# Attention of a fused attention and expert kernel: unsplit 4-byte products on halves of the array

## The chip, the cores and the metric

The kernel runs on one core of a Trainium2 chip. The metric is the device time of one execution in microseconds. A core has TensorE (PE; its weight loads are listed as PEld), VectorE (DVE), ScalarE (ACT), GpSimd (POOL) and SyncE (SP, which issues the DMAs), each with its own instruction queue.

## What is computed

```python
# q, k, v: (B=2, H=8, S=576, D=64), float32
scores = matmul(q, k.T) / sqrt(D) + bias[h]      # bias: a small network of |i - j| and i, the same for both batches
attn   = exp(scores - max);  attn /= attn.sum(-1) + 1e-9
x      = matmul(attn, v)                         # put together to (B*S=1152, H*D=512)
x = max(x @ w1, x @ w2, x @ w3) @ w_out          # first dense layers, 768 wide
P = softmax-like gate of x (8 Sinkhorn rounds over 1152 tokens and 8 experts)
out = sum_e P[:, e] * (relu(x @ w1_e) @ w2_e)    # 8 experts, 1024 wide
```

All of it is held to nearly float32 precision. The kernel gets there by splitting operands: hi is the operand rounded to float32r, lo is the rest, and a product is the sum of two or three products of such halves.

## The kernel before

Stages follow one another: the bias table (loop over 36 groups of 16 rows, written to DRAM as `bias_f`), attention, the first dense layers (`m1_mm`, L661), their output product (L1037), the gate (L1082 is its product) and the experts (L1186, L1276), which fill the time from some 380 us on. Every engine runs its instructions in the order in which the program gives them (`manual_schedule`); the loops below therefore fix the order of each queue.

Attention goes through 72 units, 9 per head: unit k < 8 is query block k // 2 (128 rows) of batch k % 2, unit 8 is the last 64 rows of both batches. In step s of the loop (L691) these follow: `u_qk(s)` (L463): scores of unit s into a tile `sc`, two halves of 288 keys. The stationary operand `qs` holds q hi on rows 0 to 63 of the array and q lo on rows 64 to 127, so that one matmul with `kh` and one with `kl` per key half do the whole product. `u_tr(s - 3)` (L557) transposes four key blocks of 128 of the exponentials through TensorE into `pt`, `u_trl` (L565) the last 64 keys, the key tail, into `pl`. `u_max(s - 1)` (L485, VectorE) adds the bias and takes the row maximum, `u_exp(s - 2)` (L499, ACT) the exponential and its row sum. `u_ev(s - 4)` (L578) takes `pt` apart into hi `pth` (ACT copy, L575) and lo `ptl` (VectorE subtraction, L576). `pv_mm` (L604) multiplies with `vs`, which holds v hi on 64 columns and v lo on the other 64, in 9 matmuls per batch and query half of 256 or 320 rows; `pv_ev` (L617) adds the two column halves, partly by way of a DMA and GpSimd. `prep_head` (L178, GpSimd) splits q, k and v of the next head. The row sums' inverses go through a transpose (L521) and DRAM and come back as factors for `x_out` (L644); for the last head `r_mm` (L546) spreads them over the array. `m1_first` (L668) places 36 matmuls of the dense layers into the drain of the attention loop, and `w_step` (L135) prepares their weights. For head 0, GpSimd does the splits in five pieces inside the bias loop (L430, one of them on ACT).

Tiles in flight: `sc` 2 buffers of two banks each, `pt` 2, `pl` 1, `pv` 1, `bias` 4.

Of the kernel before, what the change touches and what calls it, by code (L numbers as in the profile page):

```python
# [37 lines left out]
W_AT = (0, 3, 6)  # L38
NEARLY = (3, 3, 0, 0, 3, 0, 3)
LASTV = 2  # L40
NW2 = 0
# [14 lines left out]
def make_body(stop=None):  # L56
    def body(tc, a):
# [21 lines left out]
        with ctx, tc.manual_schedule():  # L79
# [77 lines left out]
            qs = [hp_.tile([128, B, 640], F32R, name=f"qs{p}", bufs=1) for p in range(2)]  # L157
            kt = [[hp_.tile([128, B, S], F32R, name=f"k{x}{p}", bufs=1) for x in "hl"] for p in range(2)]
            vs = [hp_.tile([128, B, 5, 128], F32R, name=f"vs{p}", bufs=1) for p in range(2)]
            for p in range(2):  # L160
                G.memset(raw(qs[p][:, 0, 576:640]), 0.0)
            raw_t = {}
            bias_t = {}

            def load_head(h, part=None):
                if h < H:
                    if not part:
                        raw_t[h] = (hp_.tile([128, 2, B, S], F32, tag="qk", name="qk"),
                                    hp_.tile([128, B, 5, D], F32, tag="vr", name="vr"))
                    qk, vr = raw_t[h]  # L170
                    if part is None:
                        dma(qk, a["qk"][h])
                    elif part < 2:
                        dma(qk[:, part], a["qk"][h][:, part])
                    if part in (None, 2):
                        dma(vr, a["v"][h])

            def prep_head(h, step, b=None, on_act=False):  # L178

                p = h % 2  # L180
                qk, vr = raw_t[h]
                bs = slice(0, B) if b is None else slice(b, b + 1)
                if step[0] == "q":
                    rows = slice(0, 128) if step[1] == "h" else slice(64, 128)
                    out = hi = qs[p][rows, bs, 0:S]
                    src = qk[rows, 0, bs]
                elif step[0] == "k":
                    out, hi = kt[p]["hl".index(step[1])][:, bs], kt[p][0][:, bs]
                    src = qk[:, 1, bs]
                else:  # L190
                    m = lambda x: x.rearrange("p b j d -> p (b j) d")
                    oh = 64 * (h % 2)
                    ol = 64 - oh
                    v = m(vs[p][:, bs])
                    hi = v[:, :, oh:oh + D]
                    out = hi if step[1] == "h" else v[:, :, ol:ol + D]
                    src = m(vr[:, bs])
                if step[1] == "l":
                    G.tensor_tensor(out=out, in0=src, in1=raw(hi), op=ALU.subtract)
                elif on_act:  # L200
                    A.activation(out=out, in_=src, func=AF.Copy)
                else:
                    pool_copy(out, src)

            def load_bias(m):
                h, it = divmod(m, 5)
# [9 lines left out]
            with ExitStack() as bctx:  # L216
# [10 lines left out]
                load_head(0)  # L227
# [185 lines left out]
                for g16 in range(NG16):  # L413
# [13 lines left out]
                    if g16 in (3, 5, 7):  # L427
                        load_head(1, (3, 5, 7).index(g16))
                    if g16 % 4 == 3 and 7 < g16 < 28:
                        prep_head(0, *pieces.pop(0))  # L430
# [18 lines left out]
            with ExitStack() as actx:  # L449
# [74 lines left out]
                def r_out(h):  # L524

                    A.activation(out=rt[0][0:9], in_=st_t.pop(h)[0:9, 256:384], func=AF.Copy)
                    if h == H - 1:
                        r_last.append(rt[0])
                        return
# [839 lines left out]
```

## Time and profile before

| | us |
|---|---|
| median of 3 runs (1098.21 to 1100.75) | 1099.62 |
| profiled execution, its own time | 1099.56 |
| span of the profiled execution, first to last instruction | 1097.8 |
| bias stage, to the first score | 69.0 |
| attention loop, first score to the end of the last | 125.4 |
| drain of attention, to the first dense matmul that isn't moved ahead | 16.55 |
| TensorE busy, of the span | 1049.3 |

How to read the rows: a row of the timeline has start, duration, engine, line, operation, out<-in, the size of the stationary operand, the shape of the moving one and a count of records. Matmuls overlap in the pipeline, so their durations say less than the distance from one start to the next; a row of x4 lasts from the first start to the last end. A row of the windows has the stretch, its length, and for PE, PEld, DVE, ACT and POOL the busy time and the number of records, then the granted TensorE clock (1.00 is 2.4 GHz), the share of DMA time and GB/s. A row of the groups has, behind the count, the busy time in us and the mean ns of one, then the idle time ahead of them and what ended it.

### The profile page before, as it was taken

The page shows a single profiled execution, that of the slowest core. Times are in us where ns is not written, and L with a number is a line of the kernel's source. Part 1 is how long each engine was busy: PE and PEld are TensorE (multiplying, and loading weights), DVE is VectorE, ACT ScalarE, POOL GpSimd, SP SyncE. Part 2 cuts the span into 40 slices and gives each one's busy share as a digit, 9 for nine tenths or more (in the row PEclk, how much of TensorE's full clock was granted, in tenths as well). Part 3 has the DMA queues.
Part 4 walks back from the last instruction along what each step waited for, and adds up shares of the span by engine and source line. Part 5 has one row for each costly group of instructions (what it writes and reads, how often), then busy time and mean ns, then how long its engine had stood idle before and what let it go on. Part 6 is the DMA issues. An engine that isn't in the chain of part 4 may idle for free.

```text
span 1097.8 us, 18483 instructions
## 1 busy us (share of the span) xinstructions
PE 1049.3 (96%) x7160; PEld 737.1 (67%) x7160; DVE 799.5 (73%) x1559; ACT 587.4 (54%) x999; POOL 407.9 (37%) x286
## 2 busy tenths in 40 slices
PE   6779999999999888999999999999999999999998
PEld 3269898999989663656657557566575575665753
DVE  8999999689776678677576676675766766757633
ACT  7989889533333664544535435445454354454530
POOL 6996997122212432252313312313223124132220
PEclk8999999999999899999999999999999999999999
DMA  5888664234413121121212212212112112110002
GB/s 184 275 243 267 218 194 118 67 109 115 85 52 136 25 61 42 41 64 39 63 40 63 63 24 59 67 35 63 45 56 64 24 59 72 30 44 7 1 1 87
DMA packets 41045, 90.61 MB, mean 83 GB/s; under 512 B 8255, under 2 KB 11390, under 8 KB 40062
## 3 DMA queue, kind: packets, MB, share of 16 engines
q1 hardware_dynamic: 40814, 89.14, 28.1%
q8 instruction: 56, 0.92, 0.4%
q10 hardware_dynamic: 144, 0.29, 0.1%
q14 instruction: 31, 0.25, 0.1%
HBM read 75.33 MB, written 13.30 MB: 81 GB/s over the span
## 4 chain that ended last, share of the span: by engine, by line
PE 72%; DVE 17%; ACT 4%; issue 3%; POOL 2%; DMA 1%; DVEq 0%; ACTq 0%; SPq 0%; POOLq 0%
PE d L1276 32%; PE x L1186 12%; PE y L1186 8%; PE z L1186 8%; PE sc L476 3%; PE pv L614 2%; PE pt L562 2%; PE m L665 2%; PE o L1037 2%; POOL s L350 1%; DVE ww L117 1%; DVE ww L112 1%; DVE ww L115 1%; DVE ng L493 1%; DVE ptl L576 1%
## 5 line engine op out<-in xcount | busy, mean ns | idle before, releaser
L1276 PE MATMUL d<-w2h,hl 128*128 128x512 f16 x576 | 218.3, 379 | 0.2 <-DVE hl L1207 0.2
L1276 PE MATMUL d<-w2h,hh 128*128 128x512 f16 x576 | 218.3, 379 | 0.0
L1276 PE MATMUL d<-w2l,hh 128*128 128x512 f16 x576 | 218.3, 379 | 0.0
L1186 PEld LDWEIGHTS <-w1h 128*128 128x128 f16 x1792 | 175.9, 98 | 53.1 <-issue 5.2
L1276 PEld LDWEIGHTS <-hh 128*128 128x128 f16 x1152 | 112.8, 98 | 131.5 <-issue 0.4
L1202 ACT ACTIVATE hh<-s 128x576 f16<-128x576 f32 x128 | 87.4, 683 | 127.1 <-DVE s L1198 101.6
L945 POOL TENSOR_TENSOR w1l<-wf,w1h 128x768 f16<-128x768 f32 x32 | 55.2, 1724 | 257.0 <-ACT w1h L944 239.2
L1207 DVE SCALAR_TENSOR_TENSOR hl<-s,hh 128x576 f16<-128x576 f32 x128 | 109.5, 857 | 49.1 <-ACT hh L1202 46.4
L1291 DVE SCALAR_TENSOR_TENSOR acc<-d,kh,acc 128x512 f32<-128x512 f32 x126 | 94.0, 746 | 67.3 <-PE d L1276 66.8
L1254 POOL TENSOR_TENSOR w2l<-w2r,w2h 128x512 f16<-128x512 f32 x64 | 77.1, 1214 | 117.3 <-ACT w2h L1253 117.3
L1186 PEld LDWEIGHTS <-w1l 128*128 128x128 f16 x896 | 88.3, 99 | 22.9
L1276 PEld LDWEIGHTS <-hl 128*128 128x128 f16 x576 | 56.4, 98 | 68.5 <-DVE hl L1207 0.7
L951 POOL TENSOR_TENSOR w1l<-wf,w1h 128x1024 f16<-128x1024 f32 x32 | 69.7, 2179 | 71.7 <-ACT w1h L948 71.7
L932 ACT ACTIVATE wf<-wr,pw 128x1024 f32<-128x1024 f32 x32 | 36.5, 1141 | 95.0 <-DVE pm L780 95.0
L1198 DVE SCALAR_TENSOR_TENSOR s<-z,cx,s 128x576 f32<-128x576 f32 x64 | 52.3, 817 | 44.4 <-ACT s L1194 28.3
L1194 ACT ACTIVATE s<-x,cx 128x576 f32<-128x576 f32 x96 | 70.2, 731 | 25.8 <-PE x L1186 25.7
L1186 PE MATMUL x<-xth,w1h 128*128 128x288 f16 x384 | 78.5, 286 | 1.2 <-ACT s L1194 1.2
L948 ACT ACTIVATE w1h<-wf 128x1024 f16<-128x1024 f32 x32 | 33.6, 1050 | 84.5 <-DVE wf L941 84.5
L1186 PE MATMUL x<-xth,w1l 128*128 128x288 f16 x384 | 78.7, 287 | 0.0
L1186 PE MATMUL x<-xtl,w1h 128*128 128x288 f16 x384 | 78.7, 287 | 0.0
L665 PE MATMUL m<-xh,wl 128*128 128x384 f32 x216 | 73.9, 342 | 2.5 <-POOL wl L120 2.5
L665 PE MATMUL m<-xh,wh 128*128 128x384 f32 x216 | 74.0, 343 | 1.6 <-ACT wh L119 0.8
(220 smaller groups left out, 2368.4 us busy)
## 6 DMA issues: line engine op xcount, KB each, us to landing
wr<-in_moe_w SPq DMA_DIRECT2D x50, 512.0 KB, 4.4
w2r<-in_moe_w SPq DMA_DIRECT2D x64, 256.0 KB, 2.7
bias_f<-bo SPq DMA_DIRECT2D x36, 295.5 KB, 3.6
bias<-bias_f SPq DMA_DIRECT2D x32, 288.0 KB, 3.0
qk<-in_qk SPq DMA_DIRECT2D x7, 1152.0 KB, 6.3
wr<-in_moe_w_out SPq DMA_DIRECT2D x6, 512.0 KB, 3.6
vr<-in_v SPq DMA_DIRECT2D x8, 320.0 KB, 5.8
bias<-bias_f SPq DMA_DIRECT2D x16, 144.0 KB, 5.1
```

What stands on the lines that cost most here:

```text
L665: T.matmul(out=p[:, :TG], lhsT=ws[:, 128 * c:128 * c + 128], rhs=xs[:, c, TG * g:TG * g + TG], start=(c == 0 and n == 0), stop=(c == 3 and ...
L932: A.activation(out=t[:, 0:4], in_=w1r.pop(n), func=AF.Identity, scale=w_pow[n // 2, 1][:, 2:3])
L945: G.tensor_tensor(out=lo[:, 0:3], in0=t[:, 1:4], in1=hi[:, 0:3], op=ALU.subtract)
L951: G.tensor_tensor(out=lo[:, 3:7], in0=t[:, 4:8], in1=hi[:, 3:7], op=ALU.subtract)
L1186: T.matmul(out=ps[bank][:, s, :SH], lhsT=ws[:, i, c, :], rhs=xs[:, j, c, s * SH:s * SH + SH], start=(start and k == 0), stop=(k == 5), **kw)
L1194: A.activation(out=t, in_=src, func=AF.Identity, scale=c)
L1198: V.scalar_tensor_tensor(out=out, in0=z, scalar=scale, in1=out, op0=ALU.mult, op1=ALU.add)
L1202: A.activation(out=o, in_=src, func=AF.Relu)
L1207: V.scalar_tensor_tensor(out=l, in0=src, scalar=0.0, in1=o, op0=ALU.max, op1=ALU.subtract)
L1254: G.tensor_tensor(out=lo, in0=r, in1=hi, op=ALU.subtract)
L1276: T.matmul(out=pd, lhsT=hs[:, fh, 128 * t:128 * t + 128], rhs=ws, start=(k == 0), stop=(k == 11))
L1291: V.scalar_tensor_tensor(out=acc[:, t, :], in0=pd, scalar=kh[:, 1 + t:2 + t], in1=acc[:, t, :], op0=ALU.mult, op1=ALU.add)
```

## The change

q and k of a head are loaded once per head as one tile, batch 0 on partitions 0 to 63 and batch 1 on 64 to 127, and are used unsplit; so are v and the exponentials. The loop has 36 iterations, 9 per pair of heads, and an iteration n holds two units e: for i = n % 9 < 8 the two batches of query block i // 2 of head 2p + i % 2, for i = 8 the two heads, with the last 64 rows of both batches. Scores of the two batches stand on the two row halves of the array; outputs of the two heads on its two column halves; the key tail of v, exponentials and i = 8's scores on its quarters. Key tails are turned by a plain matmul with the identity, because their result belongs on a column half. ACT and VectorE copy the transposed exponentials in turn; nothing is split. `prep_head`, the pieces in the bias stage, the second sum of outputs and its DMAs are gone.

The diff, cut to its core:

```diff
-NEARLY = (3, 3, 0, 0, 3, 0, 3)
+NEARLY = {36: 3, 38: 3, 39: 3, 40: 3}
...
             def load_head(h, part=None):
                 if h < H:
...
+                    if part in (None, 0):
+                        qk_t[h] = hp_.tile([128, 2, S], F32, tag="qk", name="qk", bufs=4)
+                        dma(qk_t[h], a["qk"][h])
+                    if part in (None, 1):
+                        v_t[h] = hp_.tile([128, B, 5, D], F32, tag="v", name="v", bufs=4)
+                        dma(v_t[h], a["v"][h])
-            def prep_head(h, step, b=None, on_act=False):
...
-                for step in ("qh", "kh"):
-                    prep_head(0, step, on_act=True)
-                pieces = [("ql", 0), ("ql", 1), ("kl", 0), ("kl", 1), ("vh", None, True)]
...
-                    if g16 % 4 == 3 and 7 < g16 < 28:
-                        prep_head(0, *pieces.pop(0))
+                    if g16 in (3, 5, 7, 9):
+                        load_head((g16 - 3) // 2 % 2, (g16 - 3) // 4)
...
+                GW = (512, 512, 128)
+                pts = [[pt_p.tile([128, 4, w], F32, name=f"pt{g}{e}") for e in range(2)] for g, w in enumerate(GW)]
+                ptt = [pt_p.tile([128, w], F32, name=f"ptt{g}") for g, w in enumerate(GW)]
+                NP = 9 * (H // 2)
...
+                def u_qk(n):
+                    p, i = divmod(n, 9)
+                    sc = [ps_s.tile([128, 2, 512], F32, tag="sc", name="sc") for _ in range(2)]
                     for hf in range(2):
+                        ks = slice(hf * SH, hf * SH + SH)
+                        for e in range(2):
+                            if i < 8:
+                                it, r = i // 2, slice(64 * e, 64 * e + 64)
+                                qk = qk_t[2 * p + i % 2]
+                                T.matmul(out=sc[e][:, hf, :SH], lhsT=qk[r, 0, 128 * it:128 * it + 128],
+                                         rhs=qk[r, 1, ks], start=True, stop=True)
+                            else:
+                                qk = qk_t[2 * p + e]
+                                for b in range(B):
+                                    r = slice(64 * b, 64 * b + 64)
+                                    T.matmul(out=sc[e][r, hf, :SH], lhsT=qk[r, 0, 512:576], rhs=qk[r, 1, ks],
+                                             start=True, stop=True)
...
+                            out = r_last[u // 4][o, 128 * (u % 4):128 * (u % 4) + 128] if u < 8 else pl_t[0][o, 128:256]
+                            T.matmul(out=out, lhsT=ident[0:18, 9 * e + u:9 * e + u + 1].to_broadcast([18, 64]),
+                                     rhs=rt[H // 2 - 1][0:18], start=True, stop=True)
...
-                    T.transpose(pl_t[0][0:64, q:q + 128], un[u]["pe"][:, 512:576], ident)
+                    T.matmul(out=pl_t[0][64 * hh:64 * hh + 64, q:q + 128], lhsT=un[u]["pe"][:, 512:576], rhs=ident,
+                             start=True, stop=True)
...
+                def ev(eng, out, in_):
+                    if eng is A:
+                        A.activation(out=out, in_=in_, func=AF.Copy)
+                    else:
+                        V.tensor_copy(out=out, in_=in_)
...
+                def pv_mm(p, g, i0, i1):
...
+                    w = GW[g] // 2
                     for i in range(i0, i1):
+                        b, j = divmod(i, 5)
+                        for e in range(2):
+                            o = slice(64 * e, 64 * e + 64)
+                            c = slice(b * w, b * w + w)
+                            v = v_t[2 * p + e]
+                            if j < 4:
+                                T.matmul(out=ps[o, c], lhsT=v[:, b, j, :], rhs=pts[g][e][:, j, c], start=(j == 0), stop=False)
+                            else:
+                                T.matmul(out=ps[o, c], lhsT=v[o, b, 4, :], rhs=ptt[g][o, c], start=False, stop=True)
...
+                PV = {6: (0, 0, 4), 7: (0, 4, 8), 8: (0, 8, 10), 10: (1, 0, 5), 11: (1, 5, 10), 12: (2, 0, 10)}
+                PV_EV = {8: (0, A), 11: (1, V), 12: (2, A)}
+                L_EV = {5: (0, V), 9: (1, A), 10: (2, V)}
+                TAILS = {1: (), 2: (), 3: (0, 1), 4: (2,), 5: (3,), 6: (), 7: (4, 5), 8: (6,), 9: (7,), 10: (8,), 11: ()}
+                X_OUT = {16: 0, 18: 1}
...
+                for n in range(NP + 6):
+                    if n < NP:
+                        u_qk(n)
+                    if 0 <= n - 2 < NP:
+                        for e in range(2):
+                            u_tr((n - 2, e))
+                    for p, (g, i0, i1) in of(PV, n):
+                        pv_mm(p, g, i0, i1)
+                    for p, tails in of(TAILS, n):
+                        for i in tails:
+                            for e in range(2):
+                                u_trl((9 * p + i, e))
+                    for p, _ in of({11: 0}, n):
+                        r_tr(p)
+                    if 0 <= n - 2 < NP:
+                        u_ev((n - 2, 0), A)
+                    if n < NP:
+                        for e in range(2):
+                            u_max((n, e))
+                            u_exp((n, e))
+                    if 0 <= n - 2 < NP:
+                        u_ev((n - 2, 1), V)
...
+                    m1_first(NEARLY.get(n, 0))
+                    if n == NP + 2:
                         r_mm()
+                for b in range(B):
+                    x_last(b)
```

In the tables the key counts from the pair's first iteration, 9p: `PV` gives group (0 and 1: 256 query rows of each batch, 2: the last 64) and the part of its 10 products. `of` yields the pairs for which a key falls on n.

## Rows read from the trace of the kernel before

**Rows 1.** The page: span, and TensorE's busy time, share and instructions.

```profile
span 1097.8 us, 18483 instructions
...
PE 1049.3 (96%) x7160; PEld 737.1 (67%) x7160; DVE 799.5 (73%) x1559; ACT 587.4 (54%) x999; POOL 407.9 (37%) x286
```

**Rows 2.** One tile's instructions, `sc`: ns min/median/max, first and last start in us.

```profile
L476 PE MATMUL sc<-kh,qs x160: 288/297/607, 69.0 to 194.1; 128*128 128x288 f32 x160
```

**Rows 3.** Windows: heads 0, 1 and 4 of attention, and the gating product.

```profile
68.99:80.82 11.83, 11.35 (x70) 10.02 (x71) 9.95 (x23) 9.17 (x23) 9.98 (x7) 0.86 0.92 278
80.82:96.07 15.25, 15.25 (x123) 15.06 (x123) 14.63 (x34) 13.88 (x34) 9.12 (x6) 1.00 0.90 299
...
127.20:144.50 17.30, 16.04 (x123) 15.02 (x123) 16.94 (x37) 14.84 (x35) 15.35 (x11) 1.00 0.72 213
...
378.38:380.44 2.06, 2.06 (x34) 0.78 (x33) 0.76 (x1) 1.83 (x3) 0.16 (x1) 1.00 0.00 0
```

**Rows 4.** Timeline of TensorE in the attention loop, around 130 and 193 us.

```profile
129.62 0.60 PE L562 MATMUL pt<-ident,pe 128*128 128x128 f32 x4
130.05 0.27 PE L571 MATMUL pl<-ident,pe 128*64 128x128 f32 x1
...
130.63 0.28 PE L614 MATMUL pv<-ptl,vs 128*128 128x256 f32 x1
130.75 0.28 PE L614 MATMUL pv<-pth,vs 128*128 128x256 f32 x1
130.88 0.29 PE L476 MATMUL sc<-kh,qs 128*128 128x288 f32 x1
131.01 0.29 PE L476 MATMUL sc<-kl,qs 128*128 128x288 f32 x1
...
192.88 0.31 PE L614 MATMUL pv<-pth,vs 128*128 128x320 f32 x1
193.02 0.31 PE L614 MATMUL pv<-ptl,vs 128*128 128x320 f32 x1
```

**Rows 5.** Timeline of TensorE around the gating product.

```profile
378.04 0.41 PE L1186 MATMUL x<-xth,w1l 128*128 128x288 f16 x2
378.38 2.13 PE L1082 MATMUL pl<-acc,wg 128*8 128x288 f32 x32
380.44 0.42 PE L1186 MATMUL y<-xth,w1h 128*128 128x288 f16 x2
```

**Rows 6.** Timeline of TensorE at the end of the last factors' spreading.

```profile
205.47 0.38 PE L552 MATMUL pl<-rt,ident 9*128 9x128 f32 x2
205.78 0.41 PE L614 MATMUL pv<-ptl,vs 128*128 128x320 f32 x1
206.03 0.30 PE L614 MATMUL pv<-pth,vs 128*128 128x320 f32 x1
```

**Rows 7.** Groups of VectorE and ACT in the attention loop, 68.99 to 194.38.

```profile
L504 ACT ACTIVATE pe<-ng,st 128x576 f32<-128x576 f32 x70 | 54.2, 774 | 3.3 <-DVE st L493 3.2
L493 DVE CUSTOM_DVE_ANT_0 ng<-sc,bias 128x576 f32<-128x576 f32 x71 | 53.3, 751 | 1.9 <-PE sc L476 1.0
...
L576 DVE TENSOR_TENSOR ptl<-pt,pth 128x512 fp32r<-128x512 f32 x67 | 45.9, 685 | 0.3 <-ACT pth L575 0.3
...
L575 ACT ACTIVATE pth<-pt 128x512 fp32r<-128x512 f32 x68 | 40.3, 593 | 8.5 <-PE pt L562 7.6
```

**Rows 8.** Waits in the attention loop: total us, times, longest us.

```profile
PEld sc L476 <- DVE st L493: 5.2, 10, 1.1
```

**Rows 9.** Waits in the bias stage, 12 to 69 us.

```profile
PE p L375 <- POOL s L350: 12.0, 21, 1.8
...
DVE t L384 <- PE p L375: 2.3, 3, 1.2
```

**Rows 10.** Timeline of TensorE: the last score, the first dense matmul not moved ahead.

```profile
194.25 0.29 PE L476 MATMUL sc<-kl,qs 128*128 128x288 f32 x1
...
210.93 0.34 PE L665 MATMUL m<-xh,wh 128*128 128x384 f32 x1
```

More of the change, by code (lines that the diff above doesn't have):

```diff
@@ L155, in body @@
             hp_ = hctx.enter_context(pool("heads", bufs=2))
[L157 to L162, printed above, removed]
+            qk_t, v_t = {}, {}
             bias_t = {}
@@ L166, in load_head @@
                 if h < H:
[L167 to L176, printed above, removed]
-            def prep_head(h, step, b=None, on_act=False):
[L180 to L203, printed above, removed]
+                    if part in (None, 0):
[4 more added lines that the diff above has]
+                        dma(v_t[h], a["v"][h])
             def load_bias(m):
-                h, it = divmod(m, 5)
+                p, it, hh = m // 10, m % 10 // 2, m % 2
+                h = 2 * p + hh
                 t = hp_.tile([128, S], F32, tag="bias", name="bias", bufs=4)
@@ L506, in u_exp @@
+                    A.activation(out=pe, in_=w.pop("ng"), func=AF.Exp, bias=st_t[p][:, 0, c:c + 1], scale=-1.0,
+                                 accum_out=st_t[p][:, 1, c:c + 1])
                     w["pe"] = pe
[L508 to L514 removed]
@@ new lines, in r_inv, with r_tr, r_out @@
+                def r_inv(p):
+                    rt[p] = up.tile([128, 128], F32, tag="rt", name="rt", bufs=1)
+                    V.tensor_scalar(out=rt[p][:, 0:18], in0=st_t[p][:, 1, :], scalar1=1e-9, scalar2=None, op0=ALU.add)
+                    V.reciprocal(out=st_t[p][:, 1, :], in_=rt[p][:, 0:18])
+                def r_tr(p):
+                    T.transpose(pl_t[0][0:18, 256:384], st_t.pop(p)[:, 1, :], ident)
+                def r_out(p):
+                    A.activation(out=rt[p][0:18], in_=pl_t[0][0:18, 256:384], func=AF.Copy)
+                    if p < H // 2 - 1:
+                        dma(r_d[2 * p:2 * p + 2].rearrange("h t p -> (h t) p"), rt[p][0:18])
@@ L649, in x_out, with pv_ev @@
+                def pv_ev(p, g, eng):
+                    ps = pvs.pop((p, g))
+                    w = GW[g] // 2
+                    if p not in x32:
+                        x32[p] = up.tile([128, B, S], F32, tag="x32", name="x32")
+                    ev(eng, x32[p][:, :, 256 * g:256 * g + w], ps[:, :GW[g]].rearrange("p (b i) -> p b i", b=B))
+                def x_out(p, b):
+                    x, r = x32[p], r_t[p]
+                    o = xh[:, p, b * S:b * S + S]
                     G.tensor_tensor(out=x[:, b], in0=x[:, b], in1=r[:, b], op=ALU.mult)
@@ new lines, in body, with of @@
+                PV = {6: (0, 0, 4), 7: (0, 4, 8), 8: (0, 8, 10), 10: (1, 0, 5), 11: (1, 5, 10), 12: (2, 0, 10)}
[3 more added lines that the diff above has]
+                X_OUT = {16: 0, 18: 1}
+                LAST = H // 2 - 1
+                def of(table, n):
+                    for p in range(H // 2):
+                        if n - 9 * p in table:
+                            yield p, table[n - 9 * p]
```

310 lines of the change are left out of this document (92 added, 218 removed).

## Prediction

> **What bounds the kernel now.** I read the page first: TensorE is busy for 1049.3 of 1097.8 us [rows 1], so the question is what the change does to TensorE's own work, and only then what it does to waits. Then the score tiles' list gives the stage: scores start at 69.0 and the last at 194.1 [rows 2]. Cut at the heads' first scores [rows 3], an early head takes 15.25 us with TensorE busy throughout, a late one 17.30 us with TensorE busy 16.04, and the drain from the last score's end (194.25 and a slot of 0.13, 194.38) to the first matmul of the next stage that isn't moved ahead (210.93, [rows 10]) 16.55. So TensorE bounds this stage, and some microseconds a head are waits. GpSimd is busy 9.12 of 15.25 us in the early head and 15.35 of 17.30 in the late one, VectorE 14.63 and 16.94: the two engines that the change relieves are close behind, but not ahead.
>
> TensorE's prices come from start-to-start distances in the middle of the stage [rows 4]: a transpose 0.109 us (four from 129.62 to 130.05), an output matmul of 256 columns 0.12, a score matmul of 288 columns 0.132 (130.88 to 131.01), an output matmul of 320 columns 0.146. The work of the loop from 68.99 to 194.38 is then 320 score matmuls x 0.132 = 42.2, 272 transposes x 0.109 = 29.6, 67 key tails x 0.109 = 7.3, seven heads' outputs x 18 x (0.12 + 0.146) = 33.5 and eight small transposes 0.9: 113.5 of 125.4 us. The other 12 us are waits and gaps; that is all that relief of the other engines could give.
>
> **What an unsplit 4-byte matmul costs.** The gating product (L1082) is the one place where the kernel multiplies unsplit 4-byte tiles in quarters of the array's columns [rows 5]: 16 calls with 288 columns leave 32 records, so each call is two passes. They take 378.38 to 380.44. Spreading the last factors over the array (L552) shows one pass on its own: two records last 0.38, one 0.27, so a pass of 128 columns takes 0.11 us, which is 0.25 for 288 [rows 6]. 32 of those in turn would be 8 us; 2.06 were needed, so four quarters ran abreast, in 8 slots of about 0.242 (2.06 less the change of shape below). Granted clock there: 1.00 [rows 3], the 2.4 GHz level. A slot is thus 0.242 us at 288 columns, 0.215 at 256, 0.111 at 128.
>
> **The loop after the change, term by term.** 36 iterations take the place of 72 units; n is the iteration. Scores: 32 iterations x 4 slots (two key halves x two passes, the two batches abreast) plus 4 x 8 slots for the iteration of the last query rows (two heads in turn, batches on the diagonal) = 160 x 0.242 = 38.7; before 42.2. Transposes: 34 iterations x 8 x 0.109 = 29.6, as before. Key tails are now true matmuls of 128 columns, two passes each; the pair of an iteration has the same column half, so they go in turn: 14.4 (before 7.3). Outputs: a head pair is 20 half-pairs of 256 columns x 2 x 0.215 = 8.6, and 10 of 64 columns x 2 x 0.08 = 1.6 (0.08 lies between 0.055, the share of columns, and 0.111, the shortest slot seen); three pairs and the first group of the fourth: 34.9 (before 33.5). With 0.3 for the small transposes: 118.0, 4.5 more than now. The hope that one unsplit product is cheaper than several split ones isn't borne out: four cycles a column on half an array cost what two matmuls at one cost.
>
> **Changes of the array's shape** are the term that decides. Scores use row halves, transposes the whole array, outputs column halves, their fifth key block a quarter (rows and columns halved), key tails column halves. Following the loop's order, 3 to 7 changes fall in an iteration (7 in the one that does group 2 and four tails), 136 in the loop and 15 in the drain; now there are next to none. Their price: the last L1186 before the gating starts at 378.04 + 0.41 - 0.29 = 378.16, its slot ends at 378.28, the gating starts at 378.38: 0.09. Eight slots end at 380.32, the next starts at 380.44: 0.12 [rows 5]. After the spread from 9 rows the slot ends at 205.69, L614's second matmul starts at 206.03 instead of 205.84: 0.19 [rows 6]. I take the mean, 0.13: 136 x 0.13 = 17.7; ends 0.09 and 0.19. A lower end of nothing is a rival below. The Trainium skill, TensorEngine Tiling (Array Packing), Key Properties, says that a change of tiling mode, not of the tile alone, drains TensorE. By that rule each of the 151 changes pays, as I forecast; without it the sum would be that of the first rival. The rule gives no price; the rows do.
>
> **Row halves abreast** are shown by no row here: L1082 shows column quarters. The nearest bounds are 0.242 a pair (as there) and 0.484 (in turn). I take the first, since passes, loads and streams are of the same kind; the second is a rival. The Trainium skill, TensorE: Matmul & The Clock Gate, Part 3, gives 3.07x for four row tiles. By that the pair is abreast and the sum stands; in turn it would be 38.7 longer.
>
> **Waits.** Both score buffers are now filled in one iteration, so the scores of n+1 wait for both u_max of n; behind them on TensorE stand all transposes, tails and outputs. A round is then at least 0.97 + 2 x 0.75 = 2.5 us (u_max 751 ns, [rows 7]). The lightest iterations hold 2.28 of work and three changes, 2.67, so they cover it; iterations 0 and 1 hold only 0.97 and wait 1.5 each, iteration 2 0.5. With 1.0 for hand-overs: 4.5. Ends 2 and 9: now the score loads wait 5.2 for VectorE, the rest lies elsewhere [rows 8].
>
> **Relief, at nothing.** The hi/lo halves of the exponentials go: ACT makes 68 copies (593 ns) and VectorE 67 subtractions (685 ns) in the loop; then each does half of them, as copies [rows 7]. GpSimd's splits of q, k and v, the second sum of outputs and its six DMAs go. In an iteration of 3.9 us ACT has 0.6 + 2 x 0.77 with the row sums behind them, VectorE 2 x 0.75 + 0.7, plus at most one more eviction: covered. If cover were missing on VectorE, one eviction late costs 0.7 an iteration. On SP, q and k of a pair are half the bytes; the bias tiles are asked for three iterations (some 8 us) ahead.
>
> **Bias stage.** Four GpSimd pieces for head 0 go. GpSimd's wait by TensorE is 12.0 us, but VectorE, which is all but gapless, idles 2.3 us for it, 1.2 of that at the start [rows 9]. So 1.0 is saved; ends 0 and 2.3.
>
> **Drain.** Left for it: 16 transposes 1.7, tails 0.7, outputs of groups 1 and 2 5.9, spread 18 calls abreast in pairs 2.0, small transpose 0.1, the same 36 early matmuls 6.2: 16.6, plus 15 x 0.13 = 2.0 and 0.7 for the last scaling: 19.3 against 16.55.
>
> **Sum.** Loop 118.0 + 17.7 + 4.5 = 140.2 against 125.4: +14.8. Drain +2.75. Bias -1.0. Together +16.5 on the profiled execution's 1099.56 us (median of the runs 1099.62): **1116.0**. What follows is unchanged and shifts. Bounds: changes -6 / +9, waits -2.5 / +4.5, bias +1 / -1.3, short slots +2: 1106 to 1131.
>
> **Rivals.**
> 1. Changes of shape hide behind loads or waits: faster. All terms but the 151 changes leave 1116.0 - 19.6 = 1096.4; even is at 0.021 us a change. For: some may fall into the waits for VectorE. Against: the three prices above, one with no wait near it. With its bounds 1092 to 1103.
> 2. Row halves run in turn: +38.7, less the 3 of waits that then vanish: 1152. Against: the quarters of L1082.
> 3. The two passes of a call keep their tile, and the partner starts with the second only: one slot more for each run of pairs, 36 x 0.242 for scores and some 30 x 0.215 for outputs, +15: 1131. Against: L1082's 8 slots leave no room for it.
> 4. The granted clock falls to the 1.2 GHz level in the waits of the light iterations (0.86 in the first head now, [rows 3]), or column halves run in turn: 1170 and more.
>
> **Chances.** Forecast 0.55, rival 1 0.22, rival 2 0.13, rival 3 0.05, rival 4 0.05. A measurement tells some 0.2% from no change (2.2 us). Rival 1 splits: 0.15 below 1097.4, 0.07 within. So faster 0.15, same 0.07, slower 0.78. The range takes in rival 1 from 1093 and rival 3, and leaves out rivals 2 and 4 (0.18): 1093 to 1140.
>
> **What would show it.** The score pairs' starts: some 0.01 apart, then 0.24 (abreast), or 0.24 each (rival 2). First transpose after scores: 0.1 to 0.2 beyond the slot (changes), or none (rival 1). A head pair at some 35 to 37 us against 31 to 35 now; TensorE records nearly without gaps while ACT, VectorE and GpSimd fall well below. A pair above 44 us, or waits for u_max or evictions as the largest idle, would make the forecast wrong.

## The result, and the profile after

| | before | after |
|---|---|---|
| median of 4 runs each, us | 1098.91 (1095.67 to 1100.75) | 1112.96 (1111.87 to 1114.23) |
| ratio to before, 95% interval | | 1.0131 [1.0104, 1.0159] |
| span of the profiled execution, us | 1097.8 | 1110.5 |
| first score starts | 69.0 | 67.7 |
| last VectorE step of attention (`xl`, the lo half of the scaled outputs; "last scaling" below) starts | 213.2 | 229.0 |
| from there to the end of the span | 884.6 | 881.5 |

The changed kernel is slower by 14.4 us, 11.4 to 17.5 by the interval. The whole of it arises between the first score and the last scaling: that stretch grew from 144.2 to 161.3 us. Ahead of it 1.3 us were gained. What follows takes 3.1 us less in this pair of executions. 0.8 of that go in the dense layers ("What follows" below); behind them the distance between the two falls from 15.0 to 12.7 us, in the stretches where the granted clock of before's profiled execution fell (0.97, 0.93 and 0.97 in the 50 us from 300, 350 and 400) and after's stayed at 1.00. So the ratio of the times is the measure, not this pair. One such window of each, before and then after:

```profile
350.00:400.00 50.00, 44.34 (x343) 35.82 (x342) 36.09 (x69) 30.92 (x49) 17.86 (x13) 0.93 0.14 36
```

```profile
350.00:400.00 50.00, 45.03 (x360) 40.31 (x358) 35.58 (x68) 27.66 (x46) 19.22 (x13) 1.00 0.15 49
```

The page of after, its span and the busy time of each engine (share of the span, instructions), answers [rows 1]:

```profile
span 1110.5 us, 18666 instructions
...
PE 1074.5 (97%) x7438; PEld 708.5 (64%) x7438; DVE 759.0 (68%) x1485; ACT 550.9 (50%) x920; POOL 319.6 (29%) x229
```

VectorE, ACT and GpSimd lost 40.5, 36.5 and 88.3 us of work, TensorE gained 25.2, and TensorE is the engine that bounds. The relief happened; it was worth less than what TensorE got to do in addition.

The same by stage. Windows of after: the first three iterations, the second of them, and the second head pair. Columns: length; busy time and instructions of PE, PEld, DVE, ACT, POOL; granted clock, DMA share, GB/s. [Rows 3] answer to them:

```profile
67.74:77.76 10.02, 8.99 (x32) 5.87 (x33) 5.16 (x13) 4.14 (x11) 0.00 (x0) 0.58 0.84 265
...
69.83:72.97 3.14, 2.96 (x9) 1.80 (x9) 1.44 (x5) 1.63 (x5) 0.00 (x0) 0.50 0.85 232
...
100.74:137.28 36.54, 36.54 (x310) 23.94 (x309) 23.42 (x54) 21.04 (x52) 7.39 (x6) 1.00 0.52 149
```

A pair takes 36.5 us at granted clock 1.00 (the 2.4 GHz level), with VectorE busy for 23.4 of them; two heads before took 30.5 (twice the early head) to 34.6 (twice the late one) [rows 3]. The start is another matter: from the second iteration on the granted clock is 0.50, the 1.2 GHz level, and eight transposes with the change of shape behind them last 1.90 (75.86 to 77.76) instead of 1.02. Ahead of that TensorE had stood for 1.77 and, behind four slots (a slot is the distance from one pass's start to the next), for 0.85 us (the idle time in brackets, and who ended it):

```profile
67.74 1.24 PE L441 MATMUL sc<-qk 64*128 64x288 f32 x8 [1.77 <-DVE t L342]
69.83 2.96 PE L441 MATMUL sc<-qk 64*128 64x288 f32 x8 [0.85 <-DVE st L463]
```

A busy time of 100% of TensorE doesn't tell work from changes of shape, because matmul records overlap; that takes the starts. Timeline of TensorE around one iteration of after, and four key tails further on (start, length, line, tiles, rows*columns of the array, moving operand, count), answering [rows 4]:

```profile
145.17 1.24 PE L441 MATMUL sc<-qk 64*128 64x288 f32 x8
146.34 1.09 PE L524 MATMUL pt<-ident,pe 128*128 128x128 f32 x8
147.36 1.95 PE L569 MATMUL pv<-pt,v 128*64 128x256 f32 x16
149.24 0.65 PE L571 MATMUL pv<-ptt,v 64*64 64x256 f32 x4
149.82 0.28 PE L486 MATMUL pl<-ident,st 128*18 128x128 f32 x1
150.02 1.24 PE L441 MATMUL sc<-qk 64*128 64x288 f32 x8
...
153.97 0.66 PE L532 MATMUL pl<-ident,pe 128*64 128x128 f32 x8
154.56 1.24 PE L441 MATMUL sc<-qk 64*128 64x288 f32 x8
```

Eight score records (four calls of two passes) take 1.24 us, not 8 x 0.24: the row halves stand abreast. 16 output records take 1.88 from start to start: column halves abreast, 8 x 0.21 and a change. The iteration from 145.17 to 150.02 is 4.85 long. Its slots are 4 x 0.24 (scores), 8 x 0.109, 8 x 0.21, 2 x 0.21 and 0.11: 4.04. The other 0.81 lies on its five changes of shape: 0.16 each.

### The profile page after: what moved, and what is told of

The parts are those of the page before. It is cut to its first block, busy times and chain, and to the rows that moved or that the text cites. A ratio compares the mean times of both kernels' runs of the same rounds, so it can differ in the third digit from the quotient of the medians.

```text
span 1110.5 us, 18666 instructions
## 1 busy us (share of the span) xinstructions
PE 1074.5 (97%) x7438; PEld 708.5 (64%) x7438; DVE 759.0 (68%) x1485; ACT 550.9 (50%) x920; POOL 319.6 (29%) x229
## 4 chain that ended last, share of the span: by engine, by line
PE 74%; DVE 17%; ACT 4%; DMA 2%; issue 2%; POOL 1%; DVEq 0%; ACTq 0%; SPq 0%
PE d L1209 28%; PE x L1119 11%; PE y L1119 8%; PE z L1119 7%; PE sc L441 4%; PE pt L524 3%; PE pv L569 3%; PE p L333 2%; PE o L970 2%; DVE pk L740 2%; PE pl L532 1%; PE m L601 1%; DVE ww L109 1%; DVE ww L114 1%; DVE ww L112 1%
## 5 line engine op out<-in xcount | busy, mean ns | idle before, releaser
L865 ACT ACTIVATE wf<-wr,pw 128x1024 f32<-128x1024 f32 x32 | 36.5, 1141 | 96.1 <-DVE pm L713 96.1
L463 DVE CUSTOM_DVE_ANT_0 ng<-sc,bias 128x576 f32<-128x576 f32 x72 | 51.7, 755 | 44.4 <-ACT pe L473 25.4
L881 ACT ACTIVATE w1h<-wf 128x1024 f16<-128x1024 f32 x32 | 33.6, 1049 | 84.5 <-DVE wf L874 84.5
```

Source lines behind the costliest of these rows:

```text
L463: V.tensor_tensor_reduce(out=ng.rearrange("p (f n) -> p f n", f=2), in0=w.pop("sc")[:, :, :SH], in1=bias_t[2 * p + hh, it].rearrange("p (f ...
```

## The experiments

All are edits of the changed kernel. Since the medians of the kernel before, run beside each, differ by 2.8 us (1098.91 to 1101.74), the ratio to it is the measure; "against after" is the difference of two ratios, times 1099.

| run | what it is | ratio to before, 95% interval | against after, us | expected, us |
|---|---|---|---|---|
| after | | 1.0131 [1.0104, 1.0159] | | |
| e1 | no quarter shape | 1.0073 [1.0057, 1.0088] | -6.4 | -6 |
| e2 | two more changes an iteration | 1.0307 [1.0289, 1.0324] | +19.3 | +12 |
| e3 | batches not in turn | 1.0130 [1.0109, 1.0151] | -0.1 | +15 to +31, or 0 |
| e4 | idle GpSimd work put back | 1.0153 [1.0138, 1.0168] | +2.4 | +1.2 |
| e5 | e1, tails transposed whole | 1.0024 [1.0013, 1.0035] | -11.8 | -13 to -14 |
| e6 | e5, outputs spread | 1.0025 [1.0012, 1.0038] | -11.6 | 3 less than e5 |
| e7 | idle matmuls ahead of and in iterations 0, 1 | 1.0156 [1.0130, 1.0182] | +2.7 | -3.4 |
| e8 | e5 with those of e7 | 1.0048 [1.0034, 1.0062] | -9.1 | 2 to 3.4 less than e5 |
| e9 | idle matmuls in iterations 0, 1 alone | 1.0115 [1.0097, 1.0134] | -1.8 | -2.6 |
| e10 | e5 with those of e9 | 0.9999 [0.9986, 1.0013] | -14.5 | 1.5 less than e5 |
| e11 | e10, idle matmuls ahead into another tile | 1.0046 [1.0028, 1.0063] | -9.3 | 2.6 to 3.7 less than e5 |
| e12 | e11 with e6's spread but for the last pair | 1.0028 [1.0015, 1.0042] | -11.3 | 1.1 less than e11 |

The theory: TensorE alone bounds the loop, and what made it longer is mostly its changes of shape. The rivals: the changes are hidden and the products themselves are dearer; or the halves run abreast only because of the order of the calls.

**e1, without the quarter shape.**

```diff
-    T.matmul(out=ps[o, c], lhsT=v[o, b, 4, :], rhs=ptt[g][o, c], start=False, stop=True)
+    T.matmul(out=ps[o, c], lhsT=v[:, b, 4, :], rhs=ptt[g][:, c], start=False, stop=True)
...
+    for h in range(H):
+        v[h, 64 - 64 * (h % 2):128 - 64 * (h % 2), :, 4] = 0.0
```

> The last key block of V is filled with zeros for the other head's half, so that its product runs over all 128 rows in the same array shape as the four blocks ahead of it: the same number of passes, but some 10 changes of shape fewer for each pair of heads (40 in all). Theory (changes of shape cost about 0.15 us each and TensorE alone bounds the loop): 40 x 0.15 = 6 us less than the changed kernel, so about 1107 us, ratio to the kernel before about 1.007. Rival (changes cost nothing, the products themselves are dearer): 1113 us as the changed kernel, ratio 1.013.

Measured: 1.0073. Timeline of the iteration with group 1's first outputs, in e1 at 140.70 and in after at 142.34:

```profile
140.70 1.95 PE L569 MATMUL pv<-pt,v 128*64 128x256 f32 x16
142.48 0.60 PE L571 MATMUL pv<-ptt,v 128*64 128x256 f32 x4
142.91 0.39 PE L532 MATMUL pl<-ident,pe 128*64 128x128 f32 x4
143.23 1.24 PE L441 MATMUL sc<-qk 64*128 64x288 f32 x8
```

```profile
142.34 1.95 PE L569 MATMUL pv<-pt,v 128*64 128x256 f32 x16
144.22 0.65 PE L571 MATMUL pv<-ptt,v 64*64 64x256 f32 x4
144.80 0.44 PE L532 MATMUL pl<-ident,pe 128*64 128x128 f32 x4
```

From the outputs' start to the next scores it is 2.53 in e1 and 2.83 in after (142.34 to 145.17): the same records, two changes fewer, 0.15 each. The window of e1's second pair says the same of ten changes: 36.5 less 35.1, 0.14 each.

```profile
100.53:135.65 35.12, 35.12 (x311) 24.20 (x310) 22.81 (x54) 21.09 (x51) 7.28 (x6) 1.00 0.55 155
```

It is the changes that cost, not the quarter's products themselves: the two iterations with group 1's outputs hold the same four quarter records each, and the one that lost two changes fell from 5.11 (140.06 to 145.17 in after) to 4.81, the one that lost one from 4.85 (145.17 to 150.02) to 4.71. A change of shape isn't hidden, and here it is TensorE that sets the end. The rival falls.

**e2, the same work with 68 more changes.** `u_qk(n, e)` now issues key half e of both batches.

```diff
-    if n < NP:
-        u_qk(n)
-    if 0 <= n - 2 < NP:
-        for e in range(2):
-            u_tr((n - 2, e))
+    for e in range(2):
+        if n < NP:
+            u_qk(n, e)
+        if 0 <= n - 2 < NP:
+            u_tr((n - 2, e))
```

> The changed kernel with the same work in another order: first half of the scores, four transposes, second half of the scores, four transposes, so that 34 iterations have two more changes of the array's shape each. Theory (changes cost 0.15 us going to the transposes and 0.20 us coming back, and TensorE bounds): 34 x 0.35 = 12 us more than the changed kernel, about 1125 us, ratio to the kernel before 1.024. Rival (changes are hidden or free): 1113 us, within 2 us of the changed kernel.

Measured: 1.0307, 19 us more than after instead of 12. Timeline of TensorE in e2, one iteration from 126.42 and one from 129.55, and the weight load of batch 1's scores in the second:

```profile
126.42 0.76 PE L445 MATMUL sc<-qk 64*128 64x288 f32 x4
127.11 0.66 PE L528 MATMUL pt<-ident,pe 128*128 128x128 f32 x4
...
129.55 1.28 PE L445 MATMUL sc<-qk 64*128 64x288 f32 x4
130.75 0.66 PE L528 MATMUL pt<-ident,pe 128*128 128x128 f32 x4
```

```profile
130.07 0.29 PEld L445 LDWEIGHTS sc<-qk 64*128 64x128 f32 x2 [0.23 <-DVE st L467]
```

The first of them is 3.13 long; its twin in after, from 154.56 to 157.34, 2.78. That is 0.35 for the two added changes, to the hundredth what was expected. In the second the first key half takes 1.20 from start to start instead of 0.69: batch 1 waits for the row maximum that frees its tile and then runs alone. 11 of the 34 iterations lose 0.44 or 0.52 us that way, and the first four iterations, most of them at the low clock, about 3 us. 11.9 (34 x 0.35), 5.2 and 3 are 20; the last score starts 20.5 us later than in after. So the price of a change held, and the expectation had left out that the added order takes away the lead that covers VectorE's row maxima. By the way it shows what abreast is worth: 0.5 us for each key half that runs in turn.

**e3, the batches' scores not in turn.**

```diff
-                    for hf in range(2):
-                        ks = slice(hf * SH, hf * SH + SH)
-                        for e in range(2):
+                    for e in range(2):
+                        for hf in range(2):
+                            ks = slice(hf * SH, hf * SH + SH)
```

> The changed kernel with the two batches' scores no longer issued in turn: both halves of the keys of batch 0, then both of batch 1. If TensorE keeps the order of issue, the row halves stand side by side for one product of two at most (batch 0's second beside batch 1's first): two to four more slots of 0.242 us in each of 32 iterations, 15 to 31 us more than the changed kernel, 1128 to 1144 us, ratio 1.027 to 1.041. Rival (the queue looks ahead and pairs them anyway, or the pairing brings nothing): 1113 us, ratio 1.013.

Measured: 1.0130, no difference. By the loop above the program has batch 0's two calls and then batch 1's two; the trace doesn't say which batch a record belongs to. Timeline of e3 where such an iteration runs:

```profile
107.47 1.25 PE L441 MATMUL sc<-qk 64*128 64x288 f32 x8
```

Its second pair takes 36.57 us, as after's 36.54. Eight records in 1.25 us are four slots: batch 1's two matmuls ran beside batch 0's two, though both stand behind them in the program. So the order of the calls isn't what makes the halves abreast, and the expectation's premise (TensorE keeps the order of issue) is wrong for matmuls on different row halves. The Trainium skill, TensorE: Matmul & The Clock Gate, Part 3 ("What overlaps and what doesn't"), says that matmuls start and end in program order, without reordering. This trace differs, and the measurement decides.

**e4, idle work in the bias stage.** Its results are read by nobody.

```diff
...
+    if g16 in (11, 15, 19, 23):
+        G.tensor_tensor(out=idle, in0=l16[:, 0:S], in1=l16[:, S:TW], op=ALU.subtract)
+    if g16 == 27:
+        A.activation(out=idle2, in_=l16[:, 0:640], func=AF.Copy)
```

> The changed kernel with idle work put back into the bias stage in place of head 0's splitting: four GpSimd subtractions of 128 x 576 at the blocks 11, 15, 19, 23 and one ScalarE copy of 128 x 640 at block 27, whose results nobody reads. Theory (the bias stage ends earlier because GpSimd is relieved): the first score returns from 67.7 us to about 69.0 and the whole is 1.2 us longer than the changed kernel. Rival (the earlier first score comes from the loads or from the order of the first products, not from GpSimd): first score stays at 67.7 us, no difference.

Measured: first score 69.1, as expected. The time is 2.4 us more than after's, but the two intervals overlap, so it is the trace that the reading rests on. Waits between 12 and 69 us (engine, what it was about to do, whom it waited for: total us, times, longest), e4 and then after; [rows 9] answer to them:

```profile
PE p L335 <- POOL s L311: 10.6, 19, 1.9
```

```profile
PE p L333 <- POOL s L311: 1.3, 4, 0.4
```

Without the idle pieces TensorE's wait for GpSimd is 1.3 instead of 10.6, and the stage ends 1.4 earlier. The bias stage's relief is GpSimd's by these waits; the one ScalarE copy, put back together with the four pieces, wasn't tried alone.

**e5, the key tails of both heads in one whole transpose**, on top of e1. The copy stands behind the exponentials, the transpose behind the others and ahead of the outputs.

```diff
+    pool_copy(tl_t[k][:, 64 * hh:64 * hh + 64], pe[:, 512:576])
...
-    T.matmul(out=pl_t[0][64 * hh:64 * hh + 64, q:q + 128], lhsT=un[u]["pe"][:, 512:576], rhs=ident,
-             start=True, stop=True)
+    T.transpose(pl_t[0][:, q:q + 128], tl_t.pop((9 * p + 2 * it, b)), ident)
...
-    TAILS = {1: (), 2: (), 3: (0, 1), 4: (2,), 5: (3,), 6: (), 7: (4, 5), 8: (6,), 9: (7,), 10: (8,), 11: ()}
+    TAILS = {3: 0, 5: 1, 7: 2, 9: 3, 10: 4}
```

> As e1, and the key tails of both heads are first put side by side by GpSimd (72 copies of 64 columns), so that one plain 128 x 128 transpose, right behind the other transposes, takes the place of two tail products in the shape of the outputs. Theory: 52 changes of shape fewer than the changed kernel (40 as in e1, 12 of the tails) at 0.15 us, 8 us; tail work of some 28 slots of 0.11 us a pair gives way to 9 transposes of 0.10 us, 2.2 us a pair, 8.7 us; given back about 3 us in the light iterations, which then end with VectorE's round of some 2.55 us instead of TensorE's 2.8: 1099 to 1100 us, ratio about 1.000. Rival (changes cost nothing): 1104 to 1107 us. If VectorE's or GpSimd's queue becomes the bound in most iterations: 1107 us or more.

Measured: 1.0024 (1104.0 beside 1100.84 for the kernel before), 11.8 us less than after, 5.4 less than e1. Window of e5's third pair, and its timeline around the short iteration from 131.26:

```profile
131.26:164.83 33.57, 33.57 (x285) 22.42 (x283) 21.48 (x52) 21.25 (x53) 12.62 (x25) 1.00 0.63 177
```

```profile
131.26 1.24 PE L441 MATMUL sc<-qk 64*128 64x288 f32 x8
...
133.67 1.69 PE L441 MATMUL sc<-qk 64*128 64x288 f32 x8
135.29 1.09 PE L530 MATMUL pt<-ident,pe 128*128 128x128 f32 x8
...
146.39 0.64 PE L574 MATMUL pv<-pt,v 128*64 128x64 f32 x16
146.85 0.29 PE L576 MATMUL pv<-ptt,v 128*64 128x64 f32 x4
```

A pair fell from 35.1 (e1) to 33.6: 1.5, where work and changes promised 2.65 (2.2 and 3 x 0.15). The rest is given back where the expectation said, but more of it: the iteration from 131.26 is only 2.41 long, and the scores behind it take 1.62 from start to start instead of 1.17, because batch 1 waits for its row maximum: 0.45, and 0.67 at the other such place of the pair, 1.1 in all instead of 0.75. The rival (changes free) expected 1104 to 1107 beside 1099 for the kernel before, a ratio of 1.0045 to 1.007, which is outside the interval.

**e6, the outputs spread thinner**, on top of e5.

```diff
-    PV = {6: (0, 0, 4), 7: (0, 4, 8), 8: (0, 8, 10), 10: (1, 0, 5), 11: (1, 5, 10), 12: (2, 0, 10)}
+    PV = {6: (0, 0, 3), 7: (0, 3, 6), 8: (0, 6, 8), 9: (0, 8, 10), 10: (1, 0, 4), 11: (1, 4, 7), 12: (1, 7, 10), 13: (2, 0, 10)}
-    PV_EV = {8: (0, A), 11: (1, V), 12: (2, A)}
+    PV_EV = {9: (0, A), 12: (1, V), 13: (2, A)}
```

> As e5, with the outputs of a head pair spread over eight of nine iterations instead of six, so that fewer iterations are shorter than VectorE's round of two row maxima (2.5 us). Theory (in e5, batch 1's scores of the iterations behind the short ones start 0.45 to 0.7 us late, about 1.1 us a pair): these waits go, two iterations more pay one change of shape each (0.15 us): 0.8 us a pair, 3 us less than e5, some 1101 us, ratio about 1.000. Rival (VectorE's round, not single short iterations, holds the loop): as e5, 1104 us. If the later outputs of the last pair lengthen the drain by more than 3 us: 1105 us or more.

Measured: 1.0025, as e5. Window of its third pair, and the last scaling (tile `xl`; ns min/median/max, first and last start in us):

```profile
131.80:165.00 33.20, 33.20 (x284) 21.96 (x282) 21.96 (x52) 21.37 (x53) 12.73 (x25) 1.00 0.61 179
```

```profile
L600 DVE TENSOR_TENSOR xl<-x,xh x2: 759/759/759, 216.6 to 218.8; 128x576 fp32r<-128x576 f32 x2
```

A pair is 0.37 shorter, 1.5 us in all. The larger of the two late starts is gone, 0.67, and two iterations more with outputs pay a change of shape each, 0.3. Against that the last pair's outputs come an iteration later: the last iteration starts 0.4 us earlier than in e5, the last scaling 2.5 later (216.3 there). 1.8 of the 2.5 had arisen by iteration 4 (81.46 instead of 79.69), ahead of any edit, where e6's profiled execution ran longer at the low clock (0.73 from 78 to 82 us, 1.00 in e5). Both expectations came half true: what the spread gains, the drain takes back.

**e7 to e12, the clock at the loop's start.** The windows of after had the clock at 0.50 behind the places where TensorE stands. Idle matmuls, whose result nobody reads, fill these places.

```diff
+    warm = ps_v.tile([128, 512], F32, tag="pv", name="pv")
+    def keep(m):
+        for _ in range(m):
+            T.matmul(out=warm[:, 0:128], lhsT=ident, rhs=ident, start=True, stop=True)
+    keep(7)
     for n in range(NP + 6):
         if n < NP:
             u_qk(n)
+        if n < 2:
+            keep(6)
```

> The changed kernel with idle matmuls (128 x 128 of the identity, two passes each, into a tile that nobody reads) where TensorE stands at the start of the loop: seven ahead of the first score, six behind the scores of iterations 0 and 1. Theory (of the 6.8 us that iterations 0 to 3 last longer than their work, most is the granted clock of 0.50 that follows TensorE's idle times): the clock stays at 1.00, iterations 0 to 2 take some 7.5 us instead of 10.0, iteration 3 2.8 instead of 3.6, together 3.4 us less, ratio to the kernel before about 1.010. Rival (VectorE's row maxima set the pace there, the clock is a bystander): less than 1 us, ratio 1.012 to 1.013. If the clock falls in spite of the idle work, the ratio is that of the changed kernel or above.

> e5 (no quarter shape, key tails in whole transposes) with the same idle matmuls as e7. Theory: e5 less 2 to 3.4 us, ratio to the kernel before 0.9995 to 1.0005, that is, level with it. Rival: as e5, 1.0024.

Measured: 1.0156 and 1.0048, worse than without them. Timeline of e7:

```profile
68.65 1.83 PE L631 MATMUL pv<-ident 128*128 128x128 f32 x14 [2.79 <-DVE bo L352]
70.40 1.24 PE L441 MATMUL sc<-qk 64*128 64x288 f32 x8
```

The seven ahead of the first score don't fill the gap: their tile too is one that VectorE frees only at the end of the bias stage, so they wait there and put the first score off by 2.7 us. What the clock gives (from here on it is 1.00) is lost at once: the last scaling starts at 229.1, as in after. e9 and e10 leave these seven out, and nothing else:

```diff
-    keep(7)
```

> As e7 without the seven idle matmuls ahead of the first score, which waited there for VectorE to free their tile and put the first score off from 67.7 to 70.4 us. Theory: first score at 67.7 us as in the changed kernel, clock 1.00 from the second iteration on, iterations 0 to 3 as in e7 (11.1 us instead of 13.7): last scaling starts 2.5 us earlier than in the changed kernel, ratio about 1.0107. If the 1.77 us that TensorE stands ahead of the first score are enough to bring the clock down: as the changed kernel, ratio 1.013, or above it by what the idle work costs.

> e5 with the idle matmuls behind the scores of iterations 0 and 1 alone. Theory: last scaling starts 1.5 us earlier than in e5 (214.8 us instead of 216.3), ratio to the kernel before about 1.001. If the clock falls all the same: as e5, 1.0024, or above.

Measured: 1.0115 and 0.9999. Timeline of e9, then the windows from 69.8 to 72.5 of e9 and of e10:

```profile
67.58 1.24 PE L441 MATMUL sc<-qk 64*128 64x288 f32 x8 [1.77 <-DVE t L342]
...
75.24 1.91 PE L441 MATMUL sc<-qk 64*128 64x288 f32 x8
```

```profile
69.80:72.50 2.70, 2.70 (x21) 2.19 (x21) 1.44 (x5) 1.62 (x5) 0.00 (x0) 1.00 0.92 250
```

```profile
69.80:72.50 2.70, 2.70 (x13) 2.48 (x12) 1.44 (x4) 1.57 (x4) 0.24 (x1) 0.50 0.80 218
```

In e9 the clock stays at 1.00, and the first three iterations take 7.66 us (67.58 to 75.24) instead of 10.02: the last scaling starts at 226.3, 2.7 us ahead of after. (The intervals of e9 and after overlap; the trace shows the gain, the time alone doesn't.) So the low clock is some 2.6 us of what the start costs. But after the same stand of 1.77 us e10's profiled execution has 0.50 and its last scaling at 217.9, behind e5's; its ratio is nevertheless better than e5's by 0.0025, 2.7 us. The mean granted clock of every timed execution is on record: e10's twelve average 0.9935, e5's twelve 0.9902, and the profiled one of e10 has 0.992; e10's five at 0.995 took 1097.7 to 1101.4 us, its other seven 1100.3 to 1104.3. So the clock came out higher in most of the timed executions, which would explain the ratio; that it did so at the loop's start isn't shown, and what decides is open. e11 and e12 tried to close the gap for good, with the seven in a tile that was meant to be free earlier.

```diff
+    warm0 = ps_t.tile([128, 512], F32, tag="pt", name="pt")
+    for _ in range(7):
+        T.matmul(out=warm0[:, 0:128], lhsT=ident, rhs=ident, start=True, stop=True)
```

> e10 with seven more idle matmuls ahead of the first score, into a transposes' tile, which VectorE frees a block of the bias stage earlier than the tile that e7 used, so that they fill the 1.77 us in which TensorE stands and don't put the first score off. Theory (the clock at the loop's start is set by whether TensorE stands ahead of the first score; in e10's profiled execution it fell there, in e9's not): first score at 67.7 us, clock 1.00 throughout, last scaling at 214 us instead of e5's 216.3, ratio to the kernel before 0.999 to 1.000. If they put the first score off as in e7: 1.002 or above.

> e11 with e6's spread of the outputs for the first three head pairs and e5's order for the last one, so that e6's 0.37 us a pair stays and its longer end goes: 1.1 us less than e11, ratio to the kernel before 0.998 to 0.999. Rival (the spread brings nothing by itself): as e11.

Measured: 1.0046 and 1.0028. Timeline of e11:

```profile
69.14 3.25 PE L640 MATMUL pt<-ident 128*128 128x128 f32 x14 [2.79 <-DVE bo L352]
72.32 1.24 PE L441 MATMUL sc<-qk 64*128 64x288 f32 x8
```

The tile is freed by the same VectorE instruction, the gap stays, and now the idle matmuls themselves run at the low clock: the first score is 4.6 us late. e12 is 2 us better than e11, as it would be if e6's spread gained something once the last pair is left as it was; but the two intervals overlap, so this isn't shown. No version here beats the kernel before; e10 is level with it (0.9999).

## Why the prediction was right, and where its terms were off

Predicted 1116.0 us and slower; measured 1112.96. In shifts, 16.5 us were forecast and 14.4 measured. The direction and its cause are as predicted; that the sum came so close is in part luck, since terms were off by up to 4 us both ways and cancel. Point by point:

- **What bounds.** Right. Every edit that took something from TensorE in the loop (e1, e5) showed in the whole, and every one that gave it more (e2) too. What the relief of VectorE, ACT and GpSimd was worth beside that is shown for the bias stage alone (e4). In the loop TensorE waited 3.1 us for row maxima before and 1.0 after (first rows below), and its four heads from 111.30 to 179.15 took 67.9 us, where four times the early head would be 61.0, while after's second and third pair take 36.54 and 36.55; whether relief or the longer iterations removed these waits, no run separates.
- **The products.** Right, and this is where the change's saving ends: unsplit products on halves abreast cost what the split ones on the whole array did. Two passes a call, 0.24 us a pair for scores (0.242 predicted), 0.21 for outputs (0.215). The short slots of group 2 were mis-sized: eight pairs between 146.39 and 146.85 in e5, where no change comes between, are 0.058 each, not 0.08; some 1.3 us less in the loop.
- **Row halves abreast** (taken from the nearest rows, [rows 5]): right. Rivals 2 and 3 fall with the eight score records in 1.24 us.
- **Changes of shape.** The mechanism was right, the price too low: 0.14 to 0.15 in e1, 0.35 for a way to the transposes and back in e2, 0.16 on average in the iteration shown, where 0.13 was taken as the mean of [rows 5, 6]. With 0.16 the 136 changes of the loop are 21.8 us, 4.1 more than forecast, within the ends 0.09 and 0.19. (Of the three prices from the rows before, 0.12 is none of its own: it and the slot of 0.242 were split from one distance, each by way of the other.) Rival 1 falls. The Trainium skill, TensorEngine Tiling (Array Packing), Key Properties, says that a change of mode drains TensorE. That each change costs TensorE time e1 and e2 bear out, with those prices; that it is a drain they don't show.
- **Key tails.** "In turn" was wrong where four of them stand in one iteration: the second query head of the pair uses the other column half, and the two pairs run abreast, the same looking ahead that e3 showed. In after the eight records from 153.97 are through at 154.56, where the next scores start: 0.59 with a change, four slots instead of eight. Two such iterations a pair, 0.44 each: 3.5 us less.
- **Waits, and the clock behind them.** Iterations 0 to 2 last 10.02 us and hold 4.1 of work and changes, iteration 3 is 0.9 longer than its like: 6.8 above the work, where 3.5 of the 4.5 had been put there. The idle time was forecast, not what it does to the clock: some 9.7 us from 69.83 on run at 0.50. In e9, where the clock stays up, iterations 0 to 3 take 11.1 instead of 13.7 us (67.58 to 78.69), so the clock is some 2.6 of the 6.8. The other 4.2 stay in e9, whose idle matmuls fill them; how much of that the row maxima alone would take isn't separated. Rival 4 came true in this one place (where the kernel before had 0.86 in its first head, [rows 3]); in the light iterations, where it had been feared, the clock stays at 1.00. Later on batch 1 starts 0.09 late in two iterations of nine, 0.7 in all.
- **Sum of the loop.** From the first score to the end of iteration 35's work (210.38 in after, where the drain's first transposes start) 142.6 us; 140.2 predicted. The four terms above (+4.1, -1.3, -3.5, and +3.0 for waits and clock: 6.8 and 0.7 against 4.5) come to +2.3, against 2.4 measured.
- **Drain.** 210.38 to 228.62, 18.2 us; 19.3 predicted.
- **Bias stage.** 1.3 gained; 1.0 predicted, from GpSimd, as the waits of e4 confirm.
- **"What follows is unchanged and shifts."** The step that failed, by a small amount. The first main dense matmul shifted by 17.7 us (210.93 to 228.62), 1.2 more than forecast. But before, TensorE came to the dense stage early and stood there for weights that were still being prepared, 0.74 us for `wl` (GpSimd) at 229.67 and 0.76 for `wh` (ACT) at 309.08. After, it comes later, and the same matmuls find their weights: they are 16.0 and 15.0 us later than before, no longer 17.7 (rows below). So what follows gave back 2.7 us, 1.9 of it at these two waits, and 15.0 is what the change costs behind the dense layers. What is left to the 14.4 lies within the interval.
- **Chances.** The forecast's own case came. Faster had 0.15, all of it on hidden changes of shape. (The bounds as listed add up to 1132, not 1131; nothing hangs on it.)

Rows for these points. Waits in the loop (total us, times, longest), before and after:

```profile
PE sc L476 <- DVE st L493: 3.1, 7, 0.9
```

```profile
PE sc L441 <- DVE st L463: 1.0, 2, 0.9
```

TensorE at the end of after's loop and the first main dense matmul; two dense matmuls of before and the same two of after; and the last scaling (`xl`) of before and of after.

```profile
210.38 0.87 PE L524 MATMUL pt<-ident,pe 128*128 128x128 f32 x6
...
228.62 0.34 PE L601 MATMUL m<-xh,wh 128*128 128x384 f32 x1
```

```profile
229.67 0.45 PE L665 MATMUL m<-xh,wl 128*128 128x384 f32 x1 [0.74 <-POOL wl L120]
...
309.08 0.44 PE L665 MATMUL m<-xh,wh 128*128 128x384 f32 x1 [0.76 <-ACT wh L119]
```

```profile
245.67 0.34 PE L601 MATMUL m<-xh,wl 128*128 128x384 f32 x1
...
324.05 0.44 PE L601 MATMUL m<-xh,wh 128*128 128x384 f32 x1
```

```profile
L659 DVE TENSOR_TENSOR xl<-x,xh x2: 759/864/970, 210.0 to 213.2; 128x576 fp32r<-128x576 f32 x2
```

```profile
L595 DVE TENSOR_TENSOR xl<-x,xh x2: 758/758/759, 226.8 to 229.0; 128x576 fp32r<-128x576 f32 x2
```

## What to carry to other kernels

Before you put products on parts of the array, count how often the program's order changes the array's shape and price each change from starts in a trace (here 0.14 to 0.18 us, as much as one and a half transposes): 151 of them are some 24 us at 0.16, an estimate, where the whole change cost 14. Zero padding that keeps the shape won back 6 us (e1), and with whole transposes of the tails, which also save passes, 12 of the 14 (e5). Relief on engines that don't bound is worth only what some wait for them was worth, so look for that wait first (here 1.3 us in the bias stage). A later start can remove waits in the next stage: 2.7 us of the shift were gone by the end of the dense layers.

## What the runs showed of the hardware that was not expected

- Matmuls on different halves of the array run beside each other even when they stand behind others in the program: two calls behind in e3 (eight records in 1.25 us, four slots), and across column halves in the key tails (eight records in 0.59 with a change). The order is the one of the loops; the traces don't name the batch or head of a record. Who wants two halves abreast needn't interleave the calls here; what breaks it is a wait in front of one half, 0.5 us a key half in e2.
- After a stand of 1.77 us, with the same TensorE instructions on both sides of it, the granted clock from 69.80 to 72.50 was 1.00 in e9's profiled execution and 0.50 in e10's. After a stand of 2.79 us seven idle matmuls took 1.83 us in e7 and e8 and 3.25 in e11, which differs from e8 in their tile alone. What decides wasn't found.
- The price of a change depends on where it goes: in e1 0.14 to 0.15 between halves and quarters, in e2 0.35 for the way from scores to transposes and back. Why they differ wasn't tried.
